# Block sums formed in PSUM on a seed that ScalarE writes, block differences on VectorE, four small stores placed later

## The chip, the cores and the metric

The kernel runs on one core of a Trainium2 chip. The metric is the device time of one execution in microseconds (us). Five engines work side by side, each through its own instructions in a fixed order: TensorE (PE; its weight loads are shown as PEld), VectorE (DVE), ScalarE (ACT), GpSimd (POOL) and SyncE (SP), which here only issues transfers. All transfers of this kernel are issued by SP. PSUM is the memory that TensorE accumulates into; SBUF holds the rest.

## The reference, cut to what matters

```python
attn = ...                                     # attention through 32 memory slots, heads merged to x (2304, 512)
h = np.maximum(x @ w_in, 0.0);  x = (h * h) @ w_out            # first network, d_ff 2048
p = domain_probs / domain_probs.sum(-1, keepdims=True)         # (2304, 4)
for e in range(4):                                             # second network, 4 experts, width 1024
    h = np.maximum(x @ w1[e], 0.0)
    out += p[:, e:e+1] * (h @ w2[e])
```

All of it is fp32. The kernel computes a product as three products of rounded halves (high by high, high by low, low by high).

## The kernel before, in words

**First stage** (0 to about 409 us): attention for 8 groups of heads, and the first network over five slabs of its width. `weights` (a generator, lines 252 to 299) brings the weights of both networks in pieces; the first 32 pieces come as 64-bit numbers by `load64` (L237) into two buffers (`raw`), and `from_f64` (L211) turns each into fp32, beginning on ScalarE (L217) and ending on VectorE (L226, L229). A `raw` buffer is free for the piece after next when L226 has read it. In this stage the expert shares `p_sb` are normalised on VectorE (L757 to L760), and four transfers (L764) write the shares of 1024 tokens to DRAM (`kept_p`), one per expert. Each is 4 KB and goes element by element (128 partitions by 8 values, transposed). `shares_of` (L573) reads one of them back, spread over all partitions, when the third stage needs it.

**Second stage** (about 409 to 735 us): tokens 0 to 1023 through 16 slabs of the second network, 256 wide. `second_pair` calls `first_products` (L507), which forms the four blocks 11, 12, 21 and 22 of a 2 by 2 block product from seven products (a Strassen scheme in Winograd's form) instead of eight. A product is six matmuls of 512 columns. PSUM tiles `u`, `v`, `m` (tag moe, three banks) and `t` (tag score) hold them: `b11`, then `t2`, then `t3` add up in `u`, and ScalarE copies `u` to SBUF after each (L527: u1, u2, u3); `b21` is in `v`, `t4` in `t`, `t1` and then `b22` in `m`. VectorE adds (L558): 11 = v + u1, 22 = m + u3, 21 = t + u3, 12 = m + u2. `rectified` (L500) takes the maximum with 0 and splits it into two halves, one on ScalarE (L501), one on VectorE (L502). The output products of the slab before (`second_l2`, L485, eight of six matmuls, their sums taken by VectorE at L498) are put behind `t2` and behind `t3` by `between`. In the same time `weights` prepares the next slabs: GpSimd forms sums of weight blocks (L305 to L308), ScalarE and VectorE split them (L244, L245), SP keeps the halves in DRAM (L315).

**Third stage** (about 735 us to the end): tokens 1024 to 2047 through the same 16 slabs, with the kept weights fetched again (L325). `third_blocks` uses `first_products` (adds at L590, then L593 takes the maximum and multiplies by the shares). GpSimd then forms four differences of the blocks in place (L605: t3, t1, t2, t4), and each is split later (`halved`, steps `t`) on ScalarE (L244) and VectorE (L245). Seven products of the slab before (`third_product`, L623, six matmuls each, into a tile of two banks from `ps_two`, which holds two such tiles) are added by VectorE to seven sums in SBUF (L630, 128 by 1024). The 256 tokens that remain go through `rest_l1` (L659, r0 and r1, a moe bank each) and `rest_l2` (L674, e). `STEPS` writes the order out by hand, with `p` for the next of the seven first products:

```python
    STEPS = "p m1 t p m2 t p m3 t p m7 p m5 p m6 m4 p r0 e r1 t".split()
```

so that in one slab TensorE does b11 m1 b21 m2 t1 m3 t4 m7 t2 m5 t3 m6 m4 b22 r0 e r1. `LAST` is the same for the last slab, with the sums gathered in between (L633). Then `third_plain` (L646, L650) does the last slab's output products and the results leave.

The framework places each engine's instructions when the program is built: where an earlier line of the program is not ready by its own reckoning, a later one may stand ahead of it, and between two that are ready the earlier line goes first. The order so fixed doesn't change at run time.

Of the kernel before, what the change touches and what calls it, by code (L numbers as in the profile page):

```python
# [12 lines left out]
F32 = mybir.dt.float32  # L13
# [26 lines left out]
def tile_kernel(  # L40
# [466 lines left out]
    def first_products(w, x, total):  # L507

        def block(t, c):
            return [[w[t][:, h, c * 256 + k * 128:c * 256 + (k + 1) * 128] for k in range(2)] for h in range(2)]  # L510

        a = {"b11": (0, 0), "b21": (0, 1), "t1": (2, 0), "t4": (1, 1), "t2": (2, 1), "t3": (3, 0), "b22": (3, 1)}

        def product(po, name, first=True):
            wb, xb = block(*a[name]), x[name]
            i = 0
            for k in range(2):
                for lw, rx in ((0, 0), (0, 1), (1, 0)):
                    nc.tensor.matmul(  # L519
                        po, wb[lw][k], xb[:, rx, k], start=(first and i == 0), stop=(i == 5),  # L520
                        skip_group_check=not first,
                    )
                    i += 1

        def copied(p):
            c = cp[0].tile([128, NB], F32, tag="c", name="cc")
            nc.scalar.copy(c, p)  # L527
            return c

        u, v, m, t = bank("moe"), bank("moe"), bank("moe"), bank("score")  # L530
        product(u, "b11")
        u1 = copied(u)
        yield
        product(v, "b21")
        total("11", v, u1)
        yield
        product(m, "t1")
        yield
        product(t, "t4")
        yield  # L540
        product(u, "t2", first=False)
        u2 = copied(u)
        yield
        product(u, "t3", first=False)
        u3 = copied(u)
        total("22", m, u3)
        total("21", t, u3)
        yield
        product(m, "b22", first=False)
        total("12", m, u2)  # L550
        yield

    def second_pair(s, x, between):
        g = {}

        def total(name, p, q):
            c = cp[0].tile([128, NB], F32, tag="c", name="c")
            nc.vector.tensor_tensor(out=c, in0=p, in1=q, op=ALU.add)  # L558
            g[name] = rectified(c, NB, hp3[0].tile([128, 2, NB], F32R, tag="g", name="g"))

        for i, _ in enumerate(first_products(w_two[0, s], x, total)):
# [13 lines left out]
    def third_blocks(s, x, later):  # L575
# [11 lines left out]
        def total(name, p, q):  # L587
            own = {"12": ("sa", 1), "21": ("sb", 1)}.get(name, ("c", 6))
            t = cp[0].tile([128, NB], F32, tag=own[0], name=f"c{name}", bufs=own[1])
            nc.vector.tensor_tensor(out=t, in0=p, in1=q, op=ALU.add)  # L590
            j = int(name[1]) - 1
            t3 = t.rearrange("p (a n) -> p a n", a=2)
            nc.vector.scalar_tensor_tensor(  # L593
                out=t3, in0=t3, scalar=0.0, in1=shares[:, 2 * j:2 * j + 2], op0=ALU.max, op1=ALU.mult
# [6 lines left out]
            for new, at, one, two, op in (  # L601
# [3 lines left out]
                nc.gpsimd.tensor_tensor(out=c[at], in0=c[one], in1=c[two], op=op)  # L605
                later.append(lambda new=new, t=c[at]: halved(new, t))

        return first_products(w_two[1, s], x, total), g

    STEPS = "p m1 t p m2 t p m3 t p m7 p m5 p m6 m4 p r0 e r1 t".split()  # L610
    LAST = "p m1 t p m2 t m2+m1 p m3 t p m7 p m5 m3+m5* p m6 m4 p r0 e r1 m6+m1 m7+m6 m4+m7 m3+m6 m7+m5".split()
# [5 lines left out]
    def third_product(s, g, name, ps_two):  # L617
        xb, t, o = A2[name]
        w = w_two[1, s][t]
        po = ps_two.tile([128, 2, NB], F32, tag="two", name="two")  # L620
        for a in range(2):
            for i, (lw, rx) in enumerate(((0, 0), (0, 1), (1, 0))):
                nc.tensor.matmul(  # L623
                    po[:, a], w[:, lw, o + a * 128:o + (a + 1) * 128], g[xb][:, rx], start=(i == 0), stop=(i == 2)
                )
        m = place(name)
        if s == 0:
# [25 lines left out]
    def rest_l1(s, x, f, g):  # L653
        w = w_two[1, s]
        ph = bank("moe")
# [55 lines left out]
    with tc.tile_pool(name="bdp", bufs=1) as bdp, tc.tile_pool(name="cv", bufs=1) as cv, \  # L711
# [51 lines left out]
        for e in range(E):  # L763
            nc.sync.dma_start(out=kept_p[e].rearrange("(t p) -> p t", p=128), in_=p_sb[:, 8:16, e])  # L764
# [29 lines left out]
    with tc.tile_pool(name="cp2", bufs=6) as cp2, tc.tile_pool(name="w2p", bufs=4) as w2, \  # L794
# [5 lines left out]
        next(ws)  # L800
        xr = rest()
# [27 lines left out]
        with tc.tile_pool(name="ps_two", bufs=2, space=bass.MemoryType.PSUM) as ps_two:  # L829
            rest_l1(0, xr, 0, gr)  # L830
            rest_l1(0, xr, 1, gr)
            for s in range(1, S2):
# [5 lines left out]
                for step in STEPS if s + 1 < S2 else LAST:  # L838
# [6 lines left out]
                    elif step[0] == "r":  # L845
                        rest_l1(s, xr, int(step[1]), gr_next)
# [60 lines left out]
```

## Time and profile before

| | us |
|---|---|
| median of three runs (lowest, highest) | 1152.75 (1149.8, 1153.49) |
| the profiled execution | 1153.97 |
| its span, first to last instruction | 1152.2 |
| PE busy | 1104.0 (96%) |
| DVE busy | 910.0 (79%) |
| ACT busy | 490.6 (43%) |
| POOL busy | 230.4 (20%) |
| mean granted TensorE clock | 0.995 |

The profiled execution is 1.2 us above the median; 1.8 us of it lie around the span. Matmuls are pipelined, so that the time from the start of one group of six to the start of the next says more than its busy time. A bracket at the end of a row of the timeline is the idle time of the engine before the row and what ended it.

### The profile page before, as it was taken

Reading aid. Unit: us, or ns where it says so; the run is one execution under the profiler, and the core shown is the slowest. Engines: PE = TensorE matmul, PEld = TensorE weight load, DVE = VectorE, ACT = ScalarE, POOL = GpSimd, SP = SyncE. Lnnn points to the kernel's source line nnn. Section 1 sums busy time; section 2 is a strip of 40 time slices with the busy share of each in tenths; the row PEclk is TensorE's granted clock in tenths of the full one; section 3 lists DMA queues with packets and bytes.
Section 4 is the critical chain, followed back from the end, with each engine's and each line's share of the span. In section 5 each row is a group of like instructions: output and inputs, shape, how many; then the busy total and the mean of one; then the engine's idle time right before and its main releaser. Section 6 shows DMA issues by size and latency. Waiting matters only on the chain.

```text
span 1152.2 us, 16664 instructions
## 1 busy us (share of the span) xinstructions
PE 1104.0 (96%) x6142; PEld 936.6 (81%) x6142; DVE 910.0 (79%) x1410; ACT 490.6 (43%) x1063; POOL 230.4 (20%) x210
## 2 busy tenths in 40 slices
PE   5886999999999999999999999999999999999997
PEld 2655888999999987787888888888788888878886
DVE  5995998977445777778888787958888888888887
ACT  3675767555455455434344343453222222222220
POOL 0032000001000223324334341032222222322220
PEclk9998999999999999999999999999999999999999
DMA  9674212221020067775767768365445555554422
GB/s 323 218 183 56 80 68 73 74 74 56 1 88 5 38 258 272 278 268 218 293 222 287 261 237 343 128 224 183 164 146 175 163 191 174 185 171 146 164 93 91
DMA packets 63874, 192.25 MB, mean 167 GB/s; under 512 B 10800, under 2 KB 12848, under 8 KB 63792
## 3 DMA queue, kind: packets, MB, share of 16 engines
q1 hardware_dynamic: 63792, 191.18, 48.0%
q8 instruction: 48, 0.79, 0.3%
q14 instruction: 34, 0.28, 0.1%
HBM read 119.31 MB, written 71.84 MB: 166 GB/s over the span
## 4 chain that ended last, share of the span: by engine, by line
PE 61%; DVE 17%; POOL 9%; DMA 5%; ACT 4%; issue 3%; SPq 0%; DVEq 0%; POOLq 0%; ACTq 0%
PE moe L519 12%; PE moe L393 9%; POOL c L605 7%; PE two L623 6%; PE fold L485 5%; PE moe L372 5%; DVE acc L630 4%; PE score L519 3%; PE turn L393 3%; DVE c L590 3%; PE memory L485 2%; PE turn L485 2%; DVE c L593 2%; PE score L393 2%; PE memory L393 2%
## 5 line engine op out<-in xcount | busy, mean ns | idle before, releaser
L605 POOL TENSOR_TENSOR c<-c,c 128x512 f32<-128x512 f32 x60 | 87.5, 1459 | 316.5 <-DVE c L593 313.0
L519 PE MATMUL moe<-mem,f 128*128 128x512 f32 x576 | 146.6, 390 | 0.2 <-DVE gr L502 0.2
L630 DVE TENSOR_TENSOR acc<-two,acc 128x1024 f32<-128x1024 f32 x98 | 119.4, 1219 | 24.9 <-PE two L623 24.9
L527 ACT COPY cc<-moe 128x512 f32<-128x512 f32 x96 | 55.9, 582 | 168.3 <-PE moe L519 168.0
L519 PEld LDWEIGHTS moe<-mem,f 128*128 128x128 f32 x576 | 107.0, 188 | 22.3 <-DVE gr L502 0.7
L519 PE MATMUL moe<-mem,ws 128*128 128x512 f32 x384 | 98.1, 391 | 2.4 <-DVE c L558 1.4
L485 PE MATMUL fold<-w,g 128*128 128x512 f32 x384 | 98.1, 389 | 0.5 <-DVE acc L498 0.5
L623 PE MATMUL two<-gt,f 128*128 128x512 f32 x360 | 88.9, 389 | 0.0
L519 PEld LDWEIGHTS moe<-mem,ws 128*128 128x128 f32 x384 | 71.6, 188 | 19.1 <-DVE c L558 2.9
L485 PEld LDWEIGHTS fold<-w,g 128*128 128x128 f32 x384 | 72.0, 188 | 15.9 <-DVE acc L498 0.9
L245 DVE TENSOR_TENSOR gt<-c,gt 128x512 fp32r<-128x512 f32 x60 | 72.8, 1214 | 15.2 <-ACT gt L244 11.1
L393 PE MATMUL moe<-ring,wo 128*128 128x384 f32 x432 | 80.9, 335 | 0.0
L372 PE MATMUL moe<-mem 128*128 128x288 f32 x432 | 75.0, 308 | 5.9 <-ACT mem L202 4.4
L623 PEld LDWEIGHTS two<-gt,f 128*128 128x128 f32 x360 | 67.6, 188 | 14.0
L372 PEld LDWEIGHTS moe<-mem 128*128 128x128 f32 x432 | 63.2, 193 | 18.6 <-issue 7.7
L244 ACT CAST gt<-c 128x512 fp32r<-128x512 f32 x60 | 37.4, 623 | 91.6 <-POOL c L605 91.6
L393 PEld LDWEIGHTS moe<-ring,wo 128*128 128x128 f32 x432 | 75.1, 188 | 0.0
L381 DVE TENSOR_TENSOR ring<-g,ring 128x288 fp32r<-128x288 f32 x96 | 45.0, 472 | 31.7 <-ACT ring L380 31.5
L305 POOL TENSOR_TENSOR s<-rb 128x256 f32<-128x256 f32 x16 | 12.4, 778 | 263.8 <-DMA rb<-in_wts 127.6
L502 DVE SCALAR_TENSOR_TENSOR g<-c,g 128x512 fp32r<-128x512 f32 x64 | 51.6, 826 | 13.3 <-ACT g L501 12.8
L379 ACT ACTIVATE g<-r 128x288 f32<-128x288 f32 x128 | 57.1, 446 | 1.9 <-DVE ring L381 0.4
L393 PE MATMUL moe<-gh,wo 128*128 128x288 f32 x192 | 46.2, 306 | 8.7 <-ACT acc L399 8.5
(176 smaller groups left out, 2353.7 us busy)
## 6 DMA issues: line engine op xcount, KB each, us to landing
f<-kept SPq DMA_DIRECT2D x128, 512.0 KB, 4.9
kept<-w SPq DMA_DIRECT2D x64, 512.0 KB, 2.7
kept<-ws SPq DMA_DIRECT2D x32, 512.0 KB, 3.8
kept<-mem SPq DMA_DIRECT2D x32, 512.0 KB, 2.7
raw<-in_wts SPq DMA_DIRECT2D x28, 512.0 KB, 3.3
ra<-in_wts SPq DMA_DIRECT2D x16, 512.0 KB, 6.5
rb<-in_wts SPq DMA_DIRECT2D x16, 512.0 KB, 5.7
kv<-in_kv SPq DMA_DIRECT2D x24, 256.0 KB, 6.4
```

Of the source, the lines that this page charges most:

```text
L245: nc.vector.tensor_tensor(out=t[:, 1], in0=w, in1=t[:, 0].bitcast(F32), op=ALU.subtract)
L372: nc.tensor.matmul(ph[:, :HS], folded[b][:, lw + hg, fc], atts[b][:, rx + hg, cs], start=(i == 0), stop=(i == 5))
L379: nc.scalar.activation(g, r, AF.Square)
L381: nc.vector.tensor_tensor(out=gl[:, f], in0=g, in1=gh[:, f].bitcast(F32), op=ALU.subtract)
L393: nc.tensor.matmul(po[:, :n], w[:, lw], rg[:, f], start=(i == 0), stop=(i == 3 * nf - 1))
L485: nc.tensor.matmul(po, g[f][:, lg, at:at + 128], w[:, rw], start=(i == 0), stop=(i == 3 * NF2 - 1))
L502: nc.vector.scalar_tensor_tensor(out=g[:, 1, :n], in0=c, scalar=0.0, in1=g[:, 0, :n].bitcast(F32), op0=ALU.max, op1=ALU.subtract)
L519: nc.tensor.matmul(po, wb[lw][k], xb[:, rx, k], start=(first and i == 0), stop=(i == 5), skip_group_check=not first,)
L527: nc.scalar.copy(c, p)
L605: nc.gpsimd.tensor_tensor(out=c[at], in0=c[one], in1=c[two], op=op)
L623: nc.tensor.matmul(po[:, a], w[:, lw, o + a * 128:o + (a + 1) * 128], g[xb][:, rx], start=(i == 0), stop=(i == 2))
L630: nc.vector.tensor_tensor(out=m, in0=po, in1=m, op=ALU.add)
```

## The change

- `first_products` takes `seeded`. The order of the seven products becomes b11, t1, b21, t2, t3, t4, b22. Where `seeded` holds (all slabs but the first of the second stage, and all of the third), ScalarE copies `u` after b11 into the PSUM tile `v` and `u` after t3 into the PSUM tile `t`; `b21` and `t4` then accumulate on that, and blocks 11 and 21 are there without an add. `rectified`, and L593 in the third stage, read them from PSUM.
- In `third_product`, for m2, m7 and m6 from slab 1 on, ScalarE copies the sum from SBUF into the PSUM tile, the product accumulates on it, and ScalarE copies the result back, in place of VectorE's add. m1, m3, m5 and m4 stay as they were.
- The four differences of L605 go from GpSimd to VectorE.
- r0 and r1 become one step `r` ahead of `e`, in one tile of `ps_two` in place of two moe banks.
- The four stores of L764 stand behind the first stage in the program, after two more steps of `weights`, ahead of `rest` and `shares_of(0)`.

```diff
-    def first_products(w, x, total):
+    def first_products(w, x, total, seeded):
...
-        def copied(p):
+        def copied(p, seed=None):
+            if seed is not None and seeded:
+                nc.scalar.copy(seed, p)
+                return None
             c = cp[0].tile([128, NB], F32, tag="c", name="cc")
             nc.scalar.copy(c, p)
             return c
 
-        u, v, m, t = bank("moe"), bank("moe"), bank("moe"), bank("score")
+        u, m, v, t = bank("moe"), bank("moe"), bank("moe"), bank("score")
         product(u, "b11")
-        u1 = copied(u)
-        yield
-        product(v, "b21")
-        total("11", v, u1)
+        u1 = copied(u, v)
         yield
         product(m, "t1")
         yield
-        product(t, "t4")
+        product(v, "b21", first=not seeded)
+        total("11", v, u1)
         yield
         product(u, "t2", first=False)
         u2 = copied(u)
@@
         product(u, "t3", first=False)
         u3 = copied(u)
         total("22", m, u3)
-        total("21", t, u3)
+        if seeded:
+            copied(u, t)
+        yield
+        product(t, "t4", first=not seeded)
+        total("21", t, None if seeded else u3)
         yield
         product(m, "b22", first=False)
         total("12", m, u2)
@@
         def total(name, p, q):
-            c = cp[0].tile([128, NB], F32, tag="c", name="c")
-            nc.vector.tensor_tensor(out=c, in0=p, in1=q, op=ALU.add)
+            c = p
+            if q is not None:
+                c = cp[0].tile([128, NB], F32, tag="c", name="c")
+                nc.vector.tensor_tensor(out=c, in0=p, in1=q, op=ALU.add)
             g[name] = rectified(c, NB, hp3[0].tile([128, 2, NB], F32R, tag="g", name="g"))
 
-        for i, _ in enumerate(first_products(w_two[0, s], x, total)):
+        for i, _ in enumerate(first_products(w_two[0, s], x, total, s > 0)):
@@
-            nc.vector.tensor_tensor(out=t, in0=p, in1=q, op=ALU.add)
+            if q is not None:
+                nc.vector.tensor_tensor(out=t, in0=p, in1=q, op=ALU.add)
+                p = t
...
-                out=t3, in0=t3, scalar=0.0, in1=shares[:, 2 * j:2 * j + 2], op0=ALU.max, op1=ALU.mult
+                out=t3, in0=p3, scalar=0.0, in1=shares[:, 2 * j:2 * j + 2], op0=ALU.max, op1=ALU.mult
@@
-                nc.gpsimd.tensor_tensor(out=c[at], in0=c[one], in1=c[two], op=op)
+                nc.vector.tensor_tensor(out=c[at], in0=c[one], in1=c[two], op=op)
@@
-    STEPS = "p m1 t p m2 t p m3 t p m7 p m5 p m6 m4 p r0 e r1 t".split()
+    STEPS = "p m1 t p m2 t p m3 t p m7 p m5 p m6 m4 p r e t".split()
...
+    SEEDED = ("m2", "m7", "m6")
@@
         po = ps_two.tile([128, 2, NB], F32, tag="two", name="two")
+        m = place(name)
+        seeded = s > 0 and name in SEEDED
+        if seeded:
+            nc.scalar.copy(po, m)
...
-                    po[:, a], w[:, lw, o + a * 128:o + (a + 1) * 128], g[xb][:, rx], start=(i == 0), stop=(i == 2)
+                    po[:, a], w[:, lw, o + a * 128:o + (a + 1) * 128], g[xb][:, rx],
+                    start=(i == 0 and not seeded), stop=(i == 2), skip_group_check=seeded,
                 )
-        m = place(name)
-        if s == 0:
+        if s == 0 or seeded:
             nc.scalar.copy(m, po)
         else:
             nc.vector.tensor_tensor(out=m, in0=po, in1=m, op=ALU.add)
@@
-    def rest_l1(s, x, f, g):
+    def rest_l1(s, x, f, g, two):
         w = w_two[1, s]
-        ph = bank("moe")
+        ph = two[:, f]
@@
-        for e in range(E):
-            nc.sync.dma_start(out=kept_p[e].rearrange("(t p) -> p t", p=128), in_=p_sb[:, 8:16, e])
...
         next(ws)
         next(ws)
+        for e in range(E):
+            nc.sync.dma_start(out=kept_p[e].rearrange("(t p) -> p t", p=128), in_=p_sb[:, 8:16, e])
         xr = rest()
         shares_of(0)
```

## Rows read from the trace of the kernel before

**Rows 1.** Stretches: window, length, PE, PEld, DVE, ACT, POOL busy, clock, DMA share, GB/s
```profile
100.00:110.00 10.00, 5.28 (x25) 5.28 (x26) 6.18 (x13) 5.95 (x15) 3.25 (x3) 0.55 0.16 48
...
550.00:700.00 150.00, 150.00 (x663) 124.19 (x662) 123.05 (x176) 60.74 (x108) 54.93 (x56) 1.00 0.69 262
...
850.27:1104.11 253.84, 249.75 (x1201) 208.16 (x1200) 218.23 (x261) 66.55 (x120) 58.37 (x40) 1.00 0.50 166
1104.00:1152.20 48.20, 40.87 (x194) 33.38 (x192) 37.72 (x47) 7.45 (x14) 8.24 (x5) 0.98 0.27 99
```
**Rows 2.** Waits of PE, 70 to 200 us and 700 us on: total, times, longest
```profile
PE moe L393 <- ACT acc L399: 8.5, 2, 8.3
...
PE two L623 <- DVE acc L630: 5.3, 13, 0.4
```
**Rows 3.** Timeline, first stage, about the stores: start, length, engine, line, operation
```profile
79.64 0.68 DVE L226 SCALAR_TENSOR_TENSOR cm<-raw,cm 128x512 f32<-128x512 uint32 x1
79.74 3.80 SPq L764 DMA_DIRECT2D kept_p<-p_sb  x4
...
83.65 9.82 SPq L237 DMA_DIRECT2D raw<-in_wts  x2
...
101.91 0.66 ACT L217 ACTIVATE cm<-raw 128x512 f32<-128x512 f32 x1 [7.30 <-DMA raw<-in_wts]
```
**Rows 4.** DMA issues of the page: count, size, median us from issue to landing
```profile
raw<-in_wts SPq DMA_DIRECT2D x28, 512.0 KB, 3.3
...
kept_p<-p_sb SPq DMA_DIRECT2D x4, 4.0 KB, 10.8
```
**Rows 5.** Timeline of SP, a series of loads about 61 us
```profile
60.54 0.80 SPq L115 DMA_DIRECT2D kv<-in_kv  x2
61.39 0.42 SPq L237 DMA_DIRECT2D raw<-in_wts  x1
61.91 1.42 SPq L115 DMA_DIRECT2D kv<-in_kv  x3
```
**Rows 6.** Timeline, one slab of the third stage, about m3
```profile
882.56 1.52 PE L519 MATMUL moe<-mem,f 128*128 128x512 f32 x6
883.21 1.22 DVE L630 TENSOR_TENSOR acc<-two,acc 128x1024 f32<-128x1024 f32 x1
...
884.49 1.66 PE L623 MATMUL two<-g,f 128*128 128x512 f32 x6 [0.41 <-DVE acc L630]
...
885.99 1.52 PE L519 MATMUL score<-mem,f 128*128 128x512 f32 x6
```
**Rows 7.** Groups of instructions by form: count, busy us, mean ns, idle before
```profile
L630 DVE TENSOR_TENSOR acc<-two,acc 128x1024 f32<-128x1024 f32 x98 | 119.4, 1219 | 24.9 <-PE two L623 24.9
...
L605 POOL TENSOR_TENSOR c<-c,c 128x512 f32<-128x512 f32 x60 | 87.5, 1459 | 316.5 <-DVE c L593 313.0
...
L245 DVE TENSOR_TENSOR gt<-c,gt 128x512 fp32r<-128x512 f32 x60 | 72.8, 1214 | 15.2 <-ACT gt L244 11.1
...
L590 DVE TENSOR_TENSOR c<-moe,cc 128x512 f32<-128x512 f32 x48 | 32.9, 685 | 18.8 <-ACT cc L527 18.3 <-PE moe L519 0.4
```
**Rows 8.** Timeline, ScalarE's copy of a PSUM tile of 1024, slab 0
```profile
757.40 1.01 ACT L628 COPY acc<-two 128x1024 f32<-128x1024 f32 x1
```
**Rows 9.** Timeline, one slab of the second stage, from b11 on
```profile
564.30 2.88 PE L519 MATMUL moe<-mem,w 128*128 128x512 f32 x12
...
565.91 0.68 DVE L558 TENSOR_TENSOR c<-moe,cc 128x512 f32<-128x512 f32 x1
...
566.63 0.62 ACT L244 CAST ws<-s 128x512 fp32r<-128x512 f32 x1 [0.83 <-POOL s L306]
...
567.69 0.57 ACT L527 COPY cc<-moe 128x512 f32<-128x512 f32 x1
```
**Rows 10.** Timeline, start of the second stage, t2 to t3
```profile
414.02 1.07 PE L519 MATMUL moe<-mem,w 128*128 128x512 f32 x4
414.22 0.59 ACT L527 COPY cc<-moe 128x512 f32<-128x512 f32 x1 [2.25 <-PE moe L519]
...
414.93 1.60 PE L519 MATMUL moe<-mem,ws 128*128 128x512 f32 x6
```
**Rows 11.** Timeline, the last output products
```profile
1139.23 3.02 PE L646 MATMUL two<-mem,f 128*128 128x512 f32 x12 [1.72 <-DVE acc L498]
```

More of the change, by code (lines that the diff above doesn't have):

```diff
@@ L589, in total @@
             t = cp[0].tile([128, NB], F32, tag=own[0], name=f"c{name}", bufs=own[1])
-            nc.vector.tensor_tensor(out=t, in0=p, in1=q, op=ALU.add)
+            if q is not None:
+                nc.vector.tensor_tensor(out=t, in0=p, in1=q, op=ALU.add)
+                p = t
             j = int(name[1]) - 1
-            t3 = t.rearrange("p (a n) -> p a n", a=2)
+            p3, t3 = (a.rearrange("p (a n) -> p a n", a=2) for a in (p, t))
             nc.vector.scalar_tensor_tensor(
-                out=t3, in0=t3, scalar=0.0, in1=shares[:, 2 * j:2 * j + 2], op0=ALU.max, op1=ALU.mult
+                out=t3, in0=p3, scalar=0.0, in1=shares[:, 2 * j:2 * j + 2], op0=ALU.max, op1=ALU.mult
             )
@@ L604, in total @@
             ):
-                nc.gpsimd.tensor_tensor(out=c[at], in0=c[one], in1=c[two], op=op)
+                nc.vector.tensor_tensor(out=c[at], in0=c[one], in1=c[two], op=op)
                 later.append(lambda new=new, t=c[at]: halved(new, t))
-        return first_products(w_two[1, s], x, total), g
-    STEPS = "p m1 t p m2 t p m3 t p m7 p m5 p m6 m4 p r0 e r1 t".split()
-    LAST = "p m1 t p m2 t m2+m1 p m3 t p m7 p m5 m3+m5* p m6 m4 p r0 e r1 m6+m1 m7+m6 m4+m7 m3+m6 m7+m5".split()
+        return first_products(w_two[1, s], x, total, True), g
+    STEPS = "p m1 t p m2 t p m3 t p m7 p m5 p m6 m4 p r e t".split()
+    LAST = "p m1 t p m2 t m2+m1 p m3 t p m7 p m5 m3+m5* p m6 m4 p r e m6+m1 m7+m6 m4+m7 m3+m6 m7+m5".split()
+    SEEDED = ("m2", "m7", "m6")
     A2 = {
@@ L829, in tile_kernel @@
         with tc.tile_pool(name="ps_two", bufs=2, space=bass.MemoryType.PSUM) as ps_two:
-            rest_l1(0, xr, 0, gr)
-            rest_l1(0, xr, 1, gr)
+            two = ps_two.tile([128, 2, NB], F32, tag="two", name="two")
+            rest_l1(0, xr, 0, gr, two)
+            rest_l1(0, xr, 1, gr, two)
             for s in range(1, S2):
@@ L845, in tile_kernel @@
                     elif step[0] == "r":
-                        rest_l1(s, xr, int(step[1]), gr_next)
+                        two = ps_two.tile([128, 2, NB], F32, tag="two", name="two")
+                        for f in range(NF2):
+                            rest_l1(s, xr, f, gr_next, two)
                     elif step == "e":
```

## The prediction

> **What bounds it now.** I read the stretches first [rows 1]. In the second stage (550 to 700 us) TensorE is never idle: 663 matmuls of 512 columns in 150 us, 0.226 us each, 1.36 us for a product of six. Nothing that merely relieves another engine can gain there. In the third stage ten slabs take 253.84 us, 25.38 each, and TensorE is idle for 4 us of it; VectorE is busy 86% of it. The tail is the only late stretch with much idle time (7.3 of 48.2 us). In the first stage the stretch 100 to 110 shows the opposite picture: all engines idle for half of it and the granted clock at 0.55, that is for the most part at the lower of its two levels (1.2 GHz). Then the waits of TensorE [rows 2]: one of 8.3 us in the first stage on ScalarE, and 13 in the third stage on VectorE's add L630. These two are what the change can take away.
>
> **The four stores (first stage).** SP issues them at 79.74, and the next weight piece behind them at 83.65; ScalarE stands still for it from 94.61 to 101.91 [rows 3], and TensorE with it. That piece took 18.3 us to land, where the median of its 28 is 3.3; a store of 4 KB took 10.8 [rows 4]. So a store holds the transfer queues for about (18.3 - 3.3) / 4 = 3.75 us (an estimate from these rows). The Trainium skill, "DMA: Bandwidth & Descriptors", section "Measured", gives 0.68 us of engine time for 4 KB; by that the four would cost 2.7 us, the late piece would have another cause, and this term would be 0. The landing times of this trace decide for the larger price.
>
> How far do the stores move? Later in the program means lower in priority, not a place behind the first stage: SP takes what is ready. The series of `kv` loads shows it [rows 5]: a weight piece that came free in the middle of it went in between. The buffer of the late piece is free when L226 ends at 80.32, 0.6 us after SP could start on the stores, and SP needs about 0.95 us for each (3.80 for four) [rows 3]. Before, the stores went first as the earlier lines; after, the piece should go as soon as it is free, behind one or two of them. Behind two it lands about 81 + 3.3 + 7.5 = 92, ahead of 94.61; behind three 0.9 us after it. What goes: the 8.3 us wait, and up to 2 us for matmuls at the lower clock behind it; what is late next are the other transfers of these 20 us, which still share the queues with the remaining stores. I take **-8**; bounds 0 (order unchanged) and -10.3. Nothing late waits for the stores themselves: `shares_of(0)` reads them 300 us afterwards. Were they really issued behind the first stage, 4 x 0.95 us of SP and 15 us of busy queues would fall on the second stage's start, and `shares_of` would hold SP until they land: 0 to +15 there.
>
> **The third stage.** The visible wait is at m3. Its tile is free when VectorE has added m1, and that add begins only at 883.21; the spacing of three starts, 882.56 to 885.99, is 3.43 us where two products need 2.72 [rows 6]. That is 0.71 us a slab, 13 times: **-9.2**. The cause is VectorE's queue: the four differences on GpSimd (1.46 us each) come late, and the splits L245 beside them take 1.21 us on the mean [rows 7]. For a slab the change takes from VectorE two adds (2 x 0.69) and three of seven sums (3 x 1.22), adds four differences (0.69 each, by the nearest row, L590; up to 1.21), and lets four splits go from 1.21 to about 0.69: -1.4 - 3.7 + 2.8 - 2.1 = -4.4 of 21.8 us [rows 1, 7]. m1's add is then never behind GpSimd.
>
> What it adds lies on ScalarE: one more copy of 512 (0.58) and six of 1024 (1.01 each) [rows 8], 6.6 on top of 6.7 us a slab [rows 1]. Five of these copies must be done before a product can start. m2, m7 and m6 can be seeded as soon as the product two tiles earlier is out of PSUM, two products ahead of need; b21 has t1 (and m1, m2) between it and its source. The tight one is t4: after t3, u3, the seed of t4 and perhaps m6's seed (0.58 + 0.58 + 1.01) share m5's 1.36 us, so t4 is up to 0.8 us late, unless m6 goes first. Bounds 0 and 0.8 a slab over 14 slabs, 0 to +11; I take 0.15, **+2**, since ScalarE is busy only half of the slab and the order is built for it. The merged r step costs nothing: its two maxima hide behind e (2.7 us), as they did.
>
> **The second stage.** VectorE loses two adds a slab (1.4 of about 16.7 us), ScalarE gains 0.58. No gain can come of it, as TensorE is full. Three spans shrink: b21 now waits for a copy of b11 with one product (1.36 us) between; t3 follows t2 directly and waits for u2's copy; t1 follows b11 and needs m, which VectorE reads for 12. Where the builder sees such a wait, it puts other matmuls in, as four do before t3 at 414.02, after which t3 starts 0.12 us behind the end of the copy [rows 10]. What remains is what it doesn't foresee. I take 0.15 a slab, **+2**; bounds 0, and 2.0 a slab (below).
>
> **The tail.** 1.72 us of wait on VectorE before the last output products [rows 11]; VectorE's queue there loses one sum (1.22) and two adds. I take **-1.5**, bounds 0 and -2.
>
> Sum: -8 - 9.2 + 2 + 2 - 1.5 = -14.7 on the profiled execution of 1153.97, which stands 1.2 above the median of 1152.75; so 1138 to 1139 in terms of the median, and I say **1139**.
>
> **Rivals.**
> - *The stores stay where they were.* The order goes by readiness, and if all four go out within the 0.6 us before the piece is free, nothing moves. Then the first term is 0: **1147**. For it: the gap of 0.6 us is short. Against: SP's own 0.95 us for each.
> - *Slower: in the second stage the seed of v is late on ScalarE.* In the slab at 564.30, b11 ends near 565.7, but ScalarE first splits a weight block that waits for GpSimd (566.63), and the copy of b11 ends at 568.26 [rows 9]. Today nobody needs it before VectorE's add. After, b21 would be due at 567.02, 1.24 us earlier; and t3 would wait 0.8 us for u2 (0.2 to start, 0.58 to copy). 2.0 us x 15 slabs = 30: 1139 - 2 + 30 = **1167** with the gain of the stores. It decides from 1.1 us a slab on, where it eats the 16.7 us of the other terms. For it: these very rows. Against: GpSimd's block is late because VectorE is behind, with 12's add begun only at 565.91 [rows 9], and VectorE loses its two adds ahead of this point, so that the weights run ahead; and the filling in [rows 10].
> - *The third stage trades its wait.* t4 and the seeds lose 0.65 us a slab: 1139 + 7 = **1146** with the stores' gain, **1154** without.
> - *The clock falls.* The trace has 13 waits of 0.4 us in a stage whose granted clock stays 1.00 [rows 1, 2]; it fell only in the pause of 8 us. If new waits of a microsecond brought about 2 us of the lower level each time, as that pause did, 15 slabs would cost 30 us: **1169**. The Trainium skill, "TensorE: Matmul & The Clock Gate", section "A second HAM failure mode: psum-queue depth-cycling", describes such an oscillation from short idle times between groups. By that rule this chance would be large; the rows of this case leave it 0.02.
>
> **How the numbers follow.** Forecast 0.45; stores stay 0.24; third stage trades its wait 0.12, half with the stores' gain and half without; late seeds in the second stage 0.13, of which a third is a partial loss that ends under 1158; stores at the second stage's start 0.04 (about 1150); clock 0.02. The least that the bounds allow is 1153 - 10.3 - 9.2 - 2 - 1.2, about 1130; a full set of best cases is unlikely, so the range starts at 1131. It reaches to 1158, which leaves out most of the two slow cases (0.12) and little below. 0.3% (3.5 us) is about what a measurement of this kernel can tell from no change. Faster by more: 0.45 + 0.22 + 0.05 + 0.02 = 0.74; within: 0.02 + 0.06 + 0.02 + 0.01 = 0.11; slower: 0.15.
>
> **What would show it.** Right: the weight piece issued among the stores and no wait of ScalarE on it near 95 us; clock 1.00 from 100 to 110; the slab of the third stage at 24.6 to 24.9 us without a wait on L630; VectorE near 70% there; the second stage still 20.4 us a slab. Wrong: the four stores in one row ahead of the piece; TensorE waiting for ScalarE's copies at b21, t4 or a seeded product, or for L502's read of a PSUM tile; a second stage longer than 20.6 us a slab.

## The result: 1143.1 us, and where the time went

The changed kernel takes 1143.14 us (median of 5 runs, 1140.21 to 1146.49); the kernel before, run on the same chip, 1153.49 (5 runs, 1149.80 to 1155.78). The ratio is 0.9919, its 95% interval 0.9889 to 0.9948. The forecast was 1139, in a range of 1131 to 1158, with 0.74 on a gain of over 0.3%. The profiled execution took 1143.0 us with a span of 1141.2, where the one before took 1153.97 with 1152.2. So 11.0 us of gain can be looked for in the two traces.

I cut both by three instructions that both have: the first product of the second stage, the first of the third stage, and the start of the last e but one. Each length is the difference of two start times; the line for the second stage in the changed kernel reads (timeline of PE):

```profile
399.20 1.55 PE L519 MATMUL moe<-mem,w 128*128 128x512 f32 x6
```

| stretch | before, us | after, us | gain | forecast |
|---|---|---|---|---|
| to the second stage's first product | 407.18 | 399.20 | -7.98 | -8 |
| second stage | 320.34 | 324.80 | +4.46 | +2 |
| third stage, up to the last e but one | 373.84 | 367.28 | -6.56 | -7.2 (-9.2 + 2) |
| tail | 50.84 | 49.92 | -0.92 | -1.5 |

Of the first 7.98, 1.1 is there before any changed instruction runs: the loads of `kv` that SP issued at 76.78 us are issued at 75.65. In this pair of profiles that leaves 6.9 for the stores.

The stretches that answer to [rows 1], in the same columns (the third line is ten slabs of the third stage, from e to e):

```profile
100.00:110.00 10.00, 10.00 (x65) 9.17 (x65) 7.70 (x14) 7.50 (x22) 1.44 (x1) 0.91 0.29 79
550.00:700.00 150.00, 150.00 (x660) 123.13 (x659) 107.50 (x163) 66.59 (x118) 47.76 (x57) 1.00 0.69 259
843.12:1091.28 248.16, 248.16 (x1202) 207.41 (x1201) 176.85 (x251) 129.51 (x190) 0.00 (x0) 1.00 0.52 172
1091.28:1141.20 49.92, 43.52 (x206) 35.19 (x204) 35.53 (x47) 14.28 (x22) 2.40 (x1) 0.98 0.26 95
```

The ten slabs take 24.82 us each in place of 25.38; TensorE is idle for none of it, VectorE busy 71% (86% before), ScalarE 52% (26%). From 100 to 110 us TensorE is busy throughout, at a granted clock of 0.91 where it was 0.55. TensorE's waits over the whole kernel, the longest first:

```profile
PE turn L143 <- ACT ph L134: 8.1, 2, 6.1
PE moe L519 <- ACT cc L530: 5.4, 3, 2.4
PE moe L372 <- ACT mem L202: 4.4, 3, 2.9
PE moe L393 <- ACT acc L399: 3.3, 2, 3.1
PE turn L143 <- ACT en L144: 2.5, 1, 2.5
PE two L673 <- DVE gr L502: 1.5, 1, 1.5
```

The 13 waits on the add [rows 2] are gone, and so is the 1.72 before the last output products [rows 11]. The 8.3 on ScalarE in the first stage is 3.1. New is the second line: three waits of 1.3 to 2.4 us on the copy of `u2` (L530). All three lie before t3, at 418.71, 440.50 and 462.64 us, in the first slabs of the second stage. In the stretch from 550 to 700 TensorE is as full as it was.

**The stores.** SP and ScalarE answer to [rows 3] as follows (timeline of SP, then of ScalarE):

```profile
79.25 0.34 SPq L237 DMA_DIRECT2D raw<-in_wts  x1
79.64 4.63 SPq L814 DMA_DIRECT2D kept_p<-p_sb  x4
88.25 21.12 SPq L237 DMA_DIRECT2D raw<-in_wts  x3
...
91.33 0.67 ACT L217 ACTIVATE cm<-raw 128x512 f32<-128x512 f32 x1
95.77 0.40 ACT L399 COPY acc<-moe 128x288 f32<-128x288 f32 x1 [1.96 <-remote]
```

The weight piece goes out ahead of all four stores, and L217 no longer waits for it. What is left is a wait of 1.96 us before L399, which the profile puts down to nothing on the core ("remote"); TensorE's 3.1 us are a wait for this L399. The stores themselves are not "later": they go out at 79.64, with 80 us of the first stage before them and 320 after. What they had to wait for is in the timeline of VectorE (L774 makes the shares ready, L226 frees the buffer of the piece):

```profile
78.36 0.22 DVE L774 TENSOR_TENSOR p_sb<-p_sb,p_sum 128x72 f32<-128x72 f32 x1
78.51 0.68 DVE L226 SCALAR_TENSOR_TENSOR cm<-raw,cm 128x512 f32<-128x512 uint32 x1
```

The shares were ready at 78.58, the buffer at 79.19, and SP was idle from 77.97 on: the stores stood behind the piece in an order that was fixed when the program was built. What they do to the queues can be read in the DMA view from 80 to 92 us of the changed kernel (40 slices of 0.3 us; busy tenths, then GB/s):

```profile
DMA  9424268999987978969999999969932291150002
GB/s 307 150 61 82 109 232 314 410 262 223 102 6 6 2 5 3 2 2 1 55 1 1 1 1 1 1 1 1 1 2 0 1 1 1 0 0 0 0 0 0
DMA packets 4367, 0.70 MB, mean 59 GB/s; under 512 B 4166, under 2 KB 4166, under 8 KB 4366
```

From about 83 to 89 us the queues are 90% busy or more in most slices (60 to 90% in six of 19) and move 1 to 6 GB/s, but for one slice of 55. A store of 4 KB takes 1024 numbers of 4 bytes, and the 4166 small packets are nearly all theirs (4 x 1024). So 16 KB hold the queues for some 6 us, which a price by size would not show. The next piece, issued at 88.25 behind the stores, took 14.3 us to land, where the median is 3.3; it landed at 102.6, and L217 takes it at 105.22 without a wait. So the stores still hold up a load, but one that has the time.

**The new wait.** Around the first of the three (timeline of ScalarE, GpSimd and TensorE):

```profile
416.25 0.62 ACT L244 CAST mem<-s 128x512 fp32r<-128x512 f32 x1 [2.06 <-POOL s L306]
...
417.06 0.62 ACT L244 CAST mem<-s 128x512 fp32r<-128x512 f32 x1 [0.20 <-POOL s L308]
417.59 0.59 ACT L501 ACTIVATE g<-moe 128x512 fp32r<-128x512 f32 x1
...
418.08 0.58 ACT L530 COPY cc<-moe 128x512 f32<-128x512 f32 x1
...
418.71 1.65 PE L519 MATMUL moe<-mem,ws 128*128 128x512 f32 x6 [1.33 <-ACT cc L530]
```

ScalarE works in order. It stands 2.06 us for a block of GpSimd's, casts it and the next one, does L501, and only then copies `u2`, which TensorE needs. Before the other two waits it stands for GpSimd's blocks as well (1.32 us at 435.65, 1.67 us at 461.00).

### The profile page after: what moved, and what is told of

Read it like the earlier page. It is cut to its first block, busy times and chain, and to the rows that moved or that the text cites. A ratio compares the mean times of both kernels' runs of the same rounds, so it can differ in the third digit from the quotient of the medians.

```text
span 1141.2 us, 16527 instructions
## 1 busy us (share of the span) xinstructions
PE 1101.7 (97%) x6142; PEld 934.8 (82%) x6142; DVE 827.4 (73%) x1366; ACT 589.0 (52%) x1178; POOL 132.3 (12%) x150
## 4 chain that ended last, share of the span: by engine, by line
PE 53%; DVE 2%; DMA 1%; issue 0%; ACT 0%; POOL 0%; SPq 0%; DVEq 0%; POOLq 0%
PE moe L519 18%; PE two L637 12%; PE fold L485 5%; PE two L673 4%; PE two L688 4%; PE score L519 3%; PE turn L485 3%; PE memory L485 3%; PE two L660 1%; DMA rb<-in_wts 1%; DVE acc L498 0%; DVE c L602 0%; DVE w L245 0%; DMA kept<-w 0%; DVE acc L644 0%
## 5 line engine op out<-in xcount | busy, mean ns | idle before, releaser
L644 DVE TENSOR_TENSOR acc<-two,acc 128x1024 f32<-128x1024 f32 x56 | 68.5, 1224 | 63.9 <-PE two L637 62.6
L485 PE MATMUL fold<-w,g 128*128 128x512 f32 x384 | 100.9, 389 | 0.0
L637 PE MATMUL two<-gt,f 128*128 128x512 f32 x360 | 88.9, 389 | 0.0
L485 PEld LDWEIGHTS fold<-w,g 128*128 128x128 f32 x384 | 72.1, 188 | 15.1
L637 PEld LDWEIGHTS two<-gt,f 128*128 128x128 f32 x360 | 67.6, 188 | 14.0
L642 ACT COPY acc<-two 128x1024 f32<-128x1024 f32 x49 | 49.7, 1014 | 49.6 <-PE two L637 49.6
L530 ACT COPY cc<-moe 128x512 f32<-128x512 f32 x65 | 38.1, 586 | 52.0 <-PE moe L519 52.0
L498 DVE SCALAR_TENSOR_TENSOR acc<-fold,p_sb,acc 128x512 f32<-128x512 f32 x60 | 44.7, 745 | 14.5 <-PE fold L485 14.2
L673 PEld LDWEIGHTS two<-mem,f 128*128 128x128 f32 x384 | 49.1, 191 | 7.0 <-DVE gr L502 4.9
L673 PE MATMUL two<-mem,f 128*128 128x256 f32 x384 | 51.8, 284 | 1.9 <-DVE gr L502 1.5
L647 POOL TENSOR_TENSOR acc<-acc 128x1024 f32<-128x1024 f32 x1 | 2.4, 2396 | 417.4 <-DVE acc L644 417.4
L485 PE MATMUL turn<-w,g 128*128 128x512 f32 x192 | 50.7, 391 | 0.0
```

Source lines behind the costliest of these rows:

```text
L485: nc.tensor.matmul(po, g[f][:, lg, at:at + 128], w[:, rw], start=(i == 0), stop=(i == 3 * NF2 - 1))
L498: nc.vector.scalar_tensor_tensor(out=oa, in0=po, scalar=pe, in1=oa, op0=ALU.mult, op1=ALU.add)
L637: nc.tensor.matmul(po[:, a], w[:, lw, o + a * 128:o + (a + 1) * 128], g[xb][:, rx], start=(i == 0 and not seeded), stop=(i == 2), skip_gro ...
L642: nc.scalar.copy(m, po)
L644: nc.vector.tensor_tensor(out=m, in0=po, in1=m, op=ALU.add)
L673: nc.tensor.matmul(ph[:, :NR], w[f][:, lw, k * 128:(k + 1) * 128], x[:, rx, k], start=(i == 0), stop=(i == 3 * KT - 1),)
```

## The experiments

Each kernel is one edit of the one before or of the changed one. Times are medians, beside the median of the kernel before on the same chip: 1152.15 us for the first four, 1150.37 for the next four, 1152.87 for the three after them. Stage lengths are cut as above.

| kernel | to stage 2 | stage 2 | slab of stage 3 | time | ratio to before, 95% |
|---|---|---|---|---|---|
| stores only | 398.89 | 319.84 | 25.39 | 1144.04 | 0.9929 (0.9906 to 0.9952) |
| differences only | 402.86 | 321.56 | 24.68 | 1143.23 | 0.9935 (0.9913 to 0.9958) |
| differences back | 395.45 | 326.33 | 27.02 | 1174.94 | 1.0211 (1.0179 to 1.0243) |
| second stage before | 398.90 | 320.95 | 24.82 | 1135.30 | 0.9861 (0.9833 to 0.9890) |
| no seeds | 398.40 | 320.75 | 24.68 | 1135.31 | 0.9861 (0.9839 to 0.9883) |
| output products earlier | 395.37 | 326.10 | 24.83 | 1140.60 | 0.9913 (0.9893 to 0.9933) |
| rest apart | 397.22 | 325.77 | 24.79 | 1140.27 | 0.9900 (0.9877 to 0.9923) |
| stores late | 395.63 | 327.37 | 25.01 | 1146.51 | 0.9967 (0.9953 to 0.9981) |
| second order unseeded | 396.71 | 337.75 | 24.82 | 1155.82 | 1.0031 (1.0015 to 1.0047) |
| no third seeds | 396.95 | 324.80 | 24.88 | 1140.39 | 0.9901 (0.9874 to 0.9928) |
| stores in quiet | 399.24 | 321.68 | 24.68 | 1137.14 | 0.9868 (0.9846 to 0.9889) |
| third order only | 393.64 | 320.73 | 24.83 | 1131.72 (one run) | one run; before 1152.22 |

### The parts by themselves

**Stores only**: the kernel before with the two lines of the stores moved.

> The kernel before with nothing changed but the place of the four stores. My theory (the stores held the transfer queues in front of a weight piece that ScalarE needed): the piece goes out ahead of them, the ScalarE wait of 7.3 us near 95 us is gone, the second stage's first product starts 6.5 to 8 us earlier than at 407.18, the later stages keep the length they had (second 320.3 us, third up to the last slab 373.8 us), and the time is 7 us below the kernel before, about 1146. Rival (the gain of the first stage comes from other things that moved with the recompiled order): 0 to 2 us below, about 1152.

It is 8.1 us faster. The piece goes out ahead of the stores, the second stage starts at 398.89, and the third stage keeps its 25.39 a slab and its 13 waits on L630. The stores are a part by themselves, worth the 8 us of the forecast.

**Differences only**: the kernel before, with

```
-                nc.gpsimd.tensor_tensor(out=c[at], in0=c[one], in1=c[two], op=op)
+                nc.vector.tensor_tensor(out=c[at], in0=c[one], in1=c[two], op=op)
```

> The kernel before with the four differences on VectorE and no seeds, no other edit. My theory (the m3 wait comes from GpSimd's late differences, which put m1's add behind late splits): the 13 waits on L630 go, the slab falls from 25.38 to about 24.7 us, VectorE is busy about 22.5 of it, and the time is 7 to 9 us below, about 1145. Rival (VectorE's load is the cause, only the seeds relieve it): VectorE has 2.8 us more a slab, some 90% busy, the wait at m3 stays or grows to 0.5 to 1.5 us a slab, and the time is 1153 or up to 15 us above.

8.9 us faster, and the slab falls to 24.68, less than in the changed kernel. No wait on L630 is left, though VectorE is busy 88% of the stage. The window of ten slabs, columns as above:

```profile
843.00:1090.00 247.00, 247.00 (x1203) 209.08 (x1202) 217.97 (x301) 65.56 (x121) 0.00 (x0) 1.00 0.53 172
```

Its groups by form, answering to [rows 7]:

```profile
L630 DVE TENSOR_TENSOR acc<-two,acc 128x1024 f32<-128x1024 f32 x98 | 119.6, 1220 | 29.5 <-PE two L623 29.5
L245 DVE TENSOR_TENSOR gt<-c,gt 128x512 fp32r<-128x512 f32 x60 | 41.1, 685 | 0.3 <-ACT gt L244 0.3
L605 DVE TENSOR_TENSOR c<-c,c 128x512 f32<-128x512 f32 x60 | 41.0, 684 | 0.1
```

Four differences cost VectorE 2.74 us a slab (4 x 0.684), and the four splits behind them give back 2.12 (4 x 0.53, from 1.214 to 0.685). A share of 86% had looked like the trouble; 88% without a wait shows that it was not the share. What stood ahead of m1's add at 883.21 [rows 6] in the kernel before is four splits, two of them at 1.47 us each (timeline of VectorE):

```profile
877.83 2.94 DVE L245 TENSOR_TENSOR gt<-c,gt 128x512 fp32r<-128x512 f32 x2 [0.56 <-ACT gt L244]
881.03 2.26 DVE L245 TENSOR_TENSOR gt<-c,gt 128x512 fp32r<-128x512 f32 x2
```

Here, in the slab at 870 us, only one split, of 0.68 us, stands ahead of that add. How much of the gain is the shorter split and how much the place in the queue was not tried apart.

**Differences back**: the changed kernel with the same line the other way.

> The changed kernel with the four differences back on GpSimd, seeds kept. My theory: GpSimd's blocks are late again, VectorE's splits take 1.2 us again, a wait of 0.3 to 0.7 us a slab comes back on VectorE (m3, m5 or m4), slab 25.1 to 25.5 us, time 5 to 9 us above the changed kernel, about 1150. Rival (the seeds alone relieve VectorE enough): slab 24.8 us, time within 1.5 us of 1143.

Both sizes were too small: 32 us slower than the changed kernel, a slab of 27.02. The new order, the seeds and the merged r step without the differences are worse than nothing. The wait is a new one, at the first product behind the r step (timeline; the differences on GpSimd, the splits on VectorE, the read of r's tile, the product):

```profile
902.53 6.03 POOL L614 TENSOR_TENSOR c<-c,c 128x512 f32<-128x512 f32 x4 [20.98 <-ACT gr L501]
...
904.50 4.60 DVE L245 TENSOR_TENSOR gt<-c,gt 128x512 fp32r<-128x512 f32 x3 [1.64 <-ACT gt L244]
...
909.03 0.41 DVE L502 SCALAR_TENSOR_TENSOR gr<-two,gr 128x256 fp32r<-128x256 f32 x1
909.50 1.66 PE L637 MATMUL two<-mem,f 128*128 128x512 f32 x6 [1.90 <-DVE gr L502]
```

Three splits take 4.60 us while GpSimd works; L502 comes behind them, and the merged r tile holds one of the two PSUM tiles until L502 has read it: 14 waits, 26.2 us. On this the Trainium skill, "SBUF — State Buffer", section "SBUF: two separate sides", says that VectorE, when it reads two operands from SBUF, and GpSimd take turns on one pair of ports, whole instruction by whole instruction. The trace agrees: the same split takes 1251 ns on the mean here and 685 where GpSimd has no differences.

**Second stage before**: the changed kernel, whose second stage calls the old function (order b11 b21 t1 t4 t2 t3 b22, no seeds).

> The changed kernel with the second stage's products as before (no seeds there, old order b11 b21 t1 t4 t2 t3 b22); third stage as changed. My theory (the changed second stage is 4.5 us longer because t3 waits for ScalarE's copy of u2 with no other matmuls between, in its first slabs): second stage 320 to 321 us from its first product to the third stage's first, no wait on the copy over 1 us, time 3.5 to 4.5 us below the changed kernel, about 1139. Rival (the second stage lost because it started from another state, earlier against the same weight loads): it stays 324 to 325 us long and the time stays at 1143.

The second stage is 320.95 us long, 3.85 less than in the changed kernel, as expected; the wait on the copy is down to one of 1.4, where none over 1 was expected. By the two ratios the kernel is 6.7 us below the changed one; their intervals allow 2 to 11, so the trace's 3.9 is the better number.

**No seeds**: stores and differences, nothing else.

> The kernel before with the stores moved and the differences on VectorE, and nothing else: no seed, the old order of products, r0 and r1 on either side of e. My theory (these two edits are the whole gain, and independent of each other): stages as in the two single runs, 399 + 320 + 365 + 50 us, slab of the third stage 24.68 us, time 17 us below the kernel before, about 1135, 8 us below the changed kernel. Rival (the seeds earn something in the third stage or the tail, or the two edits overlap): 1139 to 1143.

1135.31, 15.1 below its own kernel before and level with the last one. The two edits add up (the ratios of the two single runs multiply to 0.9864), and the seeds, the new order and the merged r step bring nothing on top of them. Of the versions whose time rests on several runs, this and the one before are the fastest, and this is by far the smaller change.

### Why the second stage lost

**Output products earlier**: the changed kernel; its output products of the slab before are handed out behind t2 and t4 in place of t3 and t4.

```
-            if i in (4, 5):
-                between(i - 4)
+            if i in (3, 5):
+                between(i // 5)
```

> The changed kernel with one number changed: in the second stage the output products of the slab before are handed out after t2 and after t4, in place of after t3 and t4. My theory (t3 has no other matmuls ahead of it while it waits for the copy of u2): the three waits of 1.3 to 2.4 us are gone or under 0.3 us each, the second stage takes 320.5 to 322 us in place of 324.8, the time is 3 to 4 us below the changed kernel, about 1139. Rival (the copy itself is late on ScalarE whatever is between): waits of 1 us or more stay, 324 us, 1143.

My theory of the gap failed. The waits before t3 are gone, but the stage is 326.10 us; TensorE now waits as long for the two seeds (waits of TensorE in the second stage):

```profile
PE score L519 <- ACT score L527: 3.9, 4, 1.7
PE moe L519 <- ACT moe L527: 1.8, 2, 1.1
```

**Second order unseeded**: the changed kernel with `first_products(..., False)` in the second stage.

> The changed kernel with its new order of products in the second stage, but without the two seeds there. The earlier order of the output products alone did not shorten the second stage (326.1 us): the waits moved from the copy of u2 to the seeds. If the seeds are the loss (two copies a slab that have to be in time, on an engine that stands behind casts of GpSimd's blocks), the second stage is 320.5 to 322 us, the time about 1139. If the order is (t3 right behind t2, with nothing in between), waits of 1 to 2.4 us before t3 stay, the stage is 323.5 to 325 us and the time 1142 to 1143. If each alone is enough to lose it, this looks like the second case.

Neither: 337.75 us, 13 longer than with the seeds, with 13 waits on the copy of `u2` (13.7 us) that go on through the whole stage. One of them (timeline):

```profile
611.19 0.68 DVE L565 TENSOR_TENSOR c<-moe,cc 128x512 f32<-128x512 f32 x1
611.90 0.63 ACT L501 ACTIVATE g<-c 128x512 fp32r<-128x512 f32 x1 [1.36 <-DVE c L565]
612.44 0.57 ACT L530 COPY cc<-moe 128x512 f32<-128x512 f32 x1
...
613.06 1.66 PE L519 MATMUL moe<-mem,ws 128*128 128x512 f32 x6 [1.14 <-ACT cc L530]
```

Here the copy stands behind L501, which waits for VectorE's add of block 11. With the seeds L501 reads the sum from PSUM and waits for no add. So the order is what costs (some 17 us against the old one, 337.75 - 320.8), and the seeds repair all but 4 of it. In the old order t3 needs that copy too, but TensorE waits for copies of `u` only 0.7 us in the whole stage ("no seeds"), and the stage takes 320 to 321 us with nothing to repair. There t1 and t4 stand between b21 and t2, which gives ScalarE time to have block 11 behind it. That this distance is the reason is argued and not shown: no kernel changes it alone.

### What the seeds of the third stage bring

**No third seeds**: `SEEDED = ()` in the changed kernel.

> The changed kernel without the seeds of m2, m7 and m6; VectorE adds these sums again, b21 and t4 of the third stage stay seeded. My theory (the differences on VectorE are the whole gain of the third stage; the seeds are worth nothing there and cost 0.1 us a slab): no wait on the add, VectorE 83 to 88% busy, slab 24.68 to 24.75 us, the stage 1 to 2 us shorter, 1142. Rival (with four differences on it VectorE needs this relief): the wait on the add comes back, slab 25.0 to 25.4 us, 1146 to 1151.

Neither again: no wait on the add comes back, and the slab is 24.88, not shorter but 0.06 longer. With the differences on VectorE the three seeds are worth 1.0 us in the whole stage (368.28 without them, 367.28 with them), and the tail is 0.95 shorter without them (48.97), so that nothing is left of it.

**Rest apart**: the changed kernel with `STEPS` "... p r0 e r1 t", each half in a tile of its own in the banks of the block products.

> The changed kernel with the r step as before: two halves in tiles of their own, on either side of e. The third stage's slab is 24.82 us with TensorE never idle, where the differences alone gave 24.68. If the merged r step, whose halves the scheduler mixes with e, costs these 0.14 us, the slab is 24.68 and the third stage 2 us shorter, 1141. If the seeded products cost them, the slab stays 24.82 and the time 1143.

24.79: the merged r step costs 0.03 a slab, not 0.14. But it costs 0.73 in the tail: apart, the tail takes 49.19 us, and TensorE's wait of 1.5 on L502 there is gone.

**Third order only**: the kernel without seeds, with the new order and the seeds of b21 and t4 in the third stage.

> The kernel without seeds (stores moved, differences on VectorE), and in the third stage alone the new order of the blocks' products with the seeds of b21 and t4; no seeds of m2, m7, m6, the r halves apart. The slab was 24.68 us without seeds and 24.82 in the changed kernel, 24.79 with r apart, 24.88 without the three seeds. If the new order with its two seeds costs what is left, the slab here is 24.75 to 24.80 us; if the three seeds and the merged r share it, the slab is 24.68 us.

24.83, where the expectation for this case was 24.75 to 24.80; the other case, 24.68, is out. The new order of the block products with its two seeds costs the 0.15 a slab, 2.5 us in the stage. The waits of TensorE list no cause for it (230 us busy of 230 in the window from 850), but its weight loads (PEld) do. In the changed kernel (timeline about t4: the seed of a product to come, `u3`, the seed of t4, t4's weight load, t4):

```profile
884.36 1.02 ACT L634 COPY two<-acc 128x1024 f32<-128x1024 f32 x1
885.32 0.58 ACT L530 COPY cc<-moe 128x512 f32<-128x512 f32 x1
885.79 0.59 ACT L527 COPY score<-moe 128x512 f32<-128x512 f32 x1
886.44 1.22 PEld L519 LDWEIGHTS score<-mem,f 128*128 128x128 f32 x6 [0.24 <-ACT score L527]
886.46 1.62 PE L519 MATMUL score<-mem,f 128*128 128x512 f32 x6
887.92 2.20 PE L637 MATMUL two<-gt,f 128*128 128x512 f32 x9
```

From t4's start to the next one it is 1.46 us where a product takes 1.36. The weight load waits for the seed in each of the 15 slabs, 3.6 us in all; in this last kernel 4.3, in "rest apart" 3.7, and in "no seeds", which has no seed, never. In the changed kernel 13 weight loads of r wait for L502 besides (2.8 us), in "rest apart" none: the 0.03 a slab of the merged step.

In the new order with its seeds the tail is 48.20, 2.0 shorter than in "no seeds" (50.19): of the 2.5 us that the order and its seeds cost in the stage they give back 2.0 there.

These last two kernels ("rest apart" and this one) do not form the reference's sums of seeded blocks: the halves of r, 256 columns wide, use the banks that the seeds use. The Trainium skill, "PSUM — Partial Sum Buffer", section "The four PSUM rules", says that a matmul that begins a sum clears the marks of a whole bank, that only matmuls set them, and that an unmarked element is overwritten, not added to. By that the other 256 columns lose their seed, and it is what the merged tile of r is for. The instructions and their sizes are those of the whole computation.

### How much of the first stage the stores still hold

**Stores late**: the changed kernel, whose stores read a copy made at the end of the first stage.

```
+        p_late = cp2.tile([128, 8, E], F32, tag="pl", name="p_late", bufs=1)
+        nc.scalar.copy(p_late, p_sb[:, 8:16])
         for e in range(E):
-            nc.sync.dma_start(out=kept_p[e].rearrange("(t p) -> p t", p=128), in_=p_sb[:, 8:16, e])
+            nc.sync.dma_start(out=kept_p[e].rearrange("(t p) -> p t", p=128), in_=p_late[:, :, e])
```

> The changed kernel with the four stores made from a copy of the shares that is written behind the first stage, so that they cannot go out before 395 us. My theory (the stores, still issued at 80 us, fill the queues with 4-byte packets until 95 us; ScalarE's wait of 2 us near 94 us, which the profile puts down to nothing on the core, is a load of instructions behind them): no wait of ScalarE or TensorE over 1 us from 88 to 100 us, clock 1.00 there, the first stage 3 to 5 us shorter; at the second stage's start the stores cost 0 to 4 us of late weight blocks: 1139 to 1143 in all. Rival (that wait has nothing to do with the stores): it stays, and the time is 1143 to 1147.

The first stage does what was expected: no wait near 94 us, clock 1.00 from 76 to 110, 395.63. But "output products earlier" and "third order only", whose stores still go out at about 79 us, also show the clock at 1.00 there and no wait of TensorE on ScalarE over 0.6 us, and reach the second stage at 395.37 and 393.64. So ScalarE's wait near 94 us comes and goes, and that the stores cause it is not shown. The stores go out at 376.33, 19 us sooner than was said, and beside them two of the second stage's weight blocks take 17.5 us to reach DRAM. The second stage is 327.37, 2.6 longer than in the changed kernel: 0.4 of it are longer waits, and the product behind the first of them takes 2.93 us in place of 1.65, at a granted clock of 0.83 from 410 to 420 us. That the stores are behind it is not shown. The products of L637 in the third stage take 394 ns a matmul where they took 389, for which I have no cause. Later is worse: 0.9967 against 0.9919.

**Stores in quiet**: the kernel without seeds, the copy made when the second slab's buffers of the first stage come free.

> The kernel without seeds, with the stores made from a copy of the shares that can be written only once the second slab of the first stage is done, so that they go out in the stretch of the first stage where the queues are a fifth busy. My theory (the stores at 80 us still cost the first stage 2 to 4 us, through ScalarE's wait near 94 us and the lower clock behind it): clock 1.00 from 76 to 110 us, the second stage starts at 394 to 396 us, no weight piece is late by more than its 13 us of slack, the other stages as without seeds, 1131 to 1133: the fastest kernel of this study. Rival (the fetch of weights behind the stores is late there too): a new wait of 3 to 8 us on a weight piece, 1136 to 1140.

The rival held in the time, with a smaller wait than it said. The clock is 1.00 from 74 to 110. One weight piece goes out at 154.17, ahead of the stores; the next goes out behind them, at 161.96, as soon as its buffer is free, and takes 15.5 us to land (median 3.2). ScalarE waits 2.34 us for it:

```profile
155.95 3.30 SPq L785 DMA_DIRECT2D kept_p<-p_late  x4
161.96 12.89 SPq L237 DMA_DIRECT2D raw<-in_wts  x2
177.53 0.66 ACT L217 ACTIVATE cm<-raw 128x512 f32<-128x512 f32 x1 [2.34 <-DMA raw<-in_wts]
```

TensorE then waits 3.6 us in two pieces, and the second stage starts at 399.24. A busy share of 0.23 in the queues (110 to 200 us, changed kernel) does not mean that a piece has 12 us to spare.

## Why the prediction was right, and where its terms were off

**The stores, -8: right in size.** The spread between runs of the same first stage is wide: with the piece ahead of the stores ten kernels reach the second stage at 393.64 to 399.20 us (mean 397.1 with the changed one), with the stores ahead two at 407.18 and 402.86. The mean difference is 8.0. The piece went out not "behind one or two of them" but ahead of all four, and not for the reason of the step, that SP takes what is ready: the stores were ready 0.6 us before the piece, and SP stood idle. The order was fixed at the build, and the 0.6 us that the step and its rival read from the trace do not decide it. So the size is right and the way to it in part luck. The rival that the stores stay is out by the row at 79.25. What the step missed is what came next: a wait of 3.1 us stays, the clock is 0.91 and not 1.00, and in some runs the wait isn't there.

**The third stage, -9.2 + 2: right, by its parts too, but with a cause too many.** The kernel before had its first slab without the wait, 772.08 to 796.76 between two e's, 24.68 us; its other slabs take 25.38. So the wait was worth 0.70 a slab (0.71 was said), and the new order costs 0.14 (0.15 was said, for t4 and the seeds). The place was right too: t4, the product that the step called the tight one, waits for its seed in every slab (the row at 886.44). Over the stage -6.56 came of it, 0.6 less than -7.2. But the step booked the seeds' relief of VectorE (two adds, three sums) under the gain. "Differences only" has none of it and the whole gain; the new order and its seeds are where the +2 comes from. The working had the number that says so: of -4.4 us a slab, 2.1 were the splits, and the splits are what stood ahead of m1's add.

**The second stage, +2: mis-sized, 4.46.** The rival of late seeds had the mechanism, a copy on ScalarE behind casts that wait for GpSimd, and put 1.24 us of it at b21 and 0.8 at t3, in all 15 slabs, for 30 us. It came before t3 alone, and only until GpSimd's blocks ran ahead: three waits, 5.4 us, and one of 1.1 on VectorE at 520 us, where the kernel before had 2.8 in the stage. "Where the builder sees such a wait, it puts other matmuls in" held in the first slabs too, with four to eight matmuls between t2 and t3, but they did not cover a copy that was 1.3 to 2.4 us later than that; at 607 us, with four, there is no wait. The bounds, 0 to 2.0 a slab, held it; the 0.15 a slab did not, since the loss isn't spread over slabs. And order and seeds were priced as one, where one costs 17 and the other gives 13 back.

**The tail, -1.5: -0.92.** The wait of 1.72 is gone; one of 1.51 on L502 has come, at the second r product (the group L673 <- L502 above). That is the merged r step, of which the working said that it "costs nothing": with r apart the tail is 49.19, a gain of 1.65.

**The other rivals.** "The third stage trades its wait" had the right place, t4, and too large a size: 0.14 us a slab and not 0.65. "The clock falls" did not come true, and that was close. In the changed kernel's second stage the three waits of over a microsecond leave the granted clock at 1.00 (399 to 542 us). The same three waits come in "differences back", "rest apart" and "stores late", and in each of them the clock falls behind the longest one: 0.91 from 430 to 450 us behind a wait of 2.26 and behind one of 3.39, 0.83 from 410 to 420 behind one of 2.68. So the changed kernel's 2.44 was not safe by its length. In the first stage the clock fell behind the 3.1 us, where the forecast had 1.00.

The forecast was 4 us too low: 2.5 of it in the second stage, 0.6 each in the third and the tail.

## What to carry to other kernels

Before relieving a busy engine, take out the one thing that makes its queue late: here one word in the line of the four differences gave the whole gain of the third stage (0.70 us a slab), and a share of 88% was no hindrance; a new order, five seeds and a merged step cost 0.14 a slab on top of it, and 1.64 without it. A product that a copy has to seed needs more time for the copy than one product beside it: t4 lost 0.1 us in every slab so, which only the weight loads' waits show. Where an order of products is changed so that a result can be seeded, price the order without the seeds too; the seeds may only be repairing it. A store of single numbers can hold the queues far longer than its bytes say (here 16 KB in 4096 packets for some 6 us, where a load of 512 KB lands in 3.3), and the place for it is behind the next load that somebody waits for and ahead of one that has time, which may be a few lines further down and not at the end.

## What was not expected of the hardware

- Four stores of 4 KB, as 4-byte packets, keep the queues 60 to over 90% busy at 1 to 6 GB/s for about 6 us (the DMA view above); with transfers of the second stage's weights beside them (stores late) each took 15.3 us to land.
- The same split of 128x512 took 685 ns with GpSimd at rest, 1214 and 1251 beside its differences (kernel before, differences back).
- The same first stage ended up to 5.6 us apart in different profiles (393.64 to 399.20). A wait of ScalarE near 94 us, put down to nothing on the core, makes up to 3 us of it. Its cause stays open.
- Waits of nearly one length left the granted clock at 1.00 in one kernel (2.44 us, the changed one) and were followed by the lower level in others (2.26, 2.68 and 3.39 us).
